# Filter loads issued as two half loads: attention and a long convolution on one core

## The chip, the cores and the metric

The kernel runs on one core of a Trainium2 chip. The core has a matrix engine (PE), a vector engine (DVE), a scalar engine (ACT), GpSimd (POOL) and a queue engine (SP) that here does nothing but issue DMAs. Sixteen DMA engines move the data; the code of the engines is fetched over them too. The metric is the time of one execution on the device in microseconds, as the median of several runs.

## The reference

Two independent parts, whose outputs stand side by side in the last dimension (2048 positions, 2 x 512 channels, bf16):

```
a = softmax((x Wq)(x Wk)^T * Dh**-0.5) (x Wv)  per head (32 heads of 16), joined, @ wo

k_shift[s] = sum_t k[s - (ks-1-t)] * shift_k[ks-1-t]      # 4 taps
kv = k_shift * v
y  = irfft(rfft(pad(kv)) * rfft(pad(ssm_k)))[:S]          # causal convolution, 2048 taps a channel
b  = q * (y + kv * ssm_D)
return concat([a, b], -1)
```

## The kernel before

**Attention.** There are 32 head pairs by query blocks of 512, each over 16 key tiles. PE computes scores into PSUM (line 910). ScalarE turns most of the score blocks into weights with the exponential (line 935, result in PT); DVE does the others with integer arithmetic (lines 1019, 1029 and 1036, result in RST). PE then multiplies the weights by the values (line 1128). This goes on for the whole span.

**Convolution.** No transform is used: the causal convolution is done by PE as products with Toeplitz blocks (`conv_lags`, line 1379). The reversed filter rows, with ssm_D added at lag zero, are stored once to a scratch tensor in HBM, `kz_scratch` (`kz_store`). A *filter load* reads them back so that partition p of a block of 64 partitions begins one element later than partition p-1, which lays out a Toeplitz block. Each of the 256 loads takes 2 x 64 = 128 rows of SEG + S//2 = 2112 elements of bf16, 4224 bytes, into one of the R_W = 9 slots of WR. Two loads make one *quad* of four channels; there are 128 quads, and four quads in a row are a burst of the convolution. For a quad PE issues 8 lags x 4 small matmuls, its first behind the landing of both loads (`h_wr[qd]`).

**The order of work.** The program is written out by a planner in Python that keeps an estimated clock for each engine. It decides at each step which of the pieces of work is issued next: scores, value products, projections, convolution lags. The instructions of an engine then run in exactly that order, and each waits on semaphores for what it needs. The DMAs of the filter are all issued by SP in order. `open_wr` puts a load on the list when the slot it writes is free (its last reader is done); `release` (line 1344) calls `feed_wr` when the planner's estimate of the load's end (`dma_t`, at WR_KB = 330 KB a microsecond) lies early enough before the time at which PE's next block of 256 instructions is to be there. The load is then tied to a place in PE's program: SP waits until PE has come there. The planner thus counts on a block of code being served behind loads that were issued before it was asked for.

**What the change touches.** `dma` (line 419) issues a transfer on an engine's queue, books it in the planner and returns the semaphore and the count to wait for; a transfer adds 16 to the semaphore. `feed_wr` makes the source pattern of a filter load (line 1336) and calls `dma` (line 1337). The semaphores `d_wr` go round by quad modulo 6. Other users of SP's queue around it are `spread_kv` (KV<-KV, a shift within SBUF in pieces of 128 bytes) and `load_v` (OUTA<-in_B_v_dram, pieces of 256 bytes).

Of the kernel before, what the change touches and what calls it, by code (L numbers as in the profile page):

```python
# [13 lines left out]
S = 2048  # L14
# [17 lines left out]
SEG = S // 2 + 64  # L32
LEFT = 16
LKR = LEFT + S
R_W = 9
# [129 lines left out]
WR_KB = 330  # L165
# [168 lines left out]
def bass_concat_heads__mha_block__ssm_conv_h3__prompt_kernel(  # L334
# [14 lines left out]
    kz_ap = nc.dram_tensor("kz_scratch", (C // 2, 2, 2 * SEG), BF16).ap()  # L349
# [7 lines left out]
    def sem(name):  # L357
        return enter(nc.semaphore(name))

    def sb(name, shape, dt=BF16):  # L360
        return enter(nc.sbuf_tensor(name, shape, dt))
# [8 lines left out]
    WR = sb("WR", [128, R_W, SEG + S // 2])  # L370
# [42 lines left out]
    act, dve, pool, sp = [Eng(sem(n), done) for n in ("s_act", "s_dve", "s_pool", "s_sp")]  # L413
    dma_t = [0.0]

    def at(*deps):
        return pe.at(deps)

    def dma(eng, dsem, outp, inp, deps=(), transpose=False, kb=512, rate=DMA_KB, late=4.2):
        h = dsem.add()  # L420
        start = max(eng.t, at(*deps))
        dma_t[0] = max(dma_t[0], start + late) + kb / rate
        if kb >= 256:
            pe.loads.append((start + 1.31, dma_t[0] - 0.85))
        done[(id(h[0]), h[1])] = dma_t[0]

        def fn(e):
            f = e.dma_start_transpose if transpose else e.dma_start
            f(outp, inp).then_inc(dsem.sem, 16)  # L429
        issue = kb / (rate if rate < DMA_KB else 155) if transpose else 0.55  # L430
        eng.op(fn, deps, inc=False, us=(issue, issue + 0.06))
        return h
# [41 lines left out]
    d_wr = [DmaSem(sem(f"d_wr{i}")) for i in range(6)]  # L474
# [5 lines left out]
    def load_x(sc, skip=0):  # L480
        t0, t1 = sc * 512 + skip, (sc + 1) * 512
        h_x[sc] = [dma(sp, d_x[sc], xT[:, :, t0:t1], x2[t0:t1, :], transpose=True, kb=t1 - t0, rate=X_KB, late=1.8)]
    h_xn = dma(sp, d_x[4], XN, x2[0:256, :].rearrange("(j p) f -> p j f", p=128), kb=256, late=1.8)
    h_wq = [dma(act, d_w[0], WQ[:, :, 0:128], wview[:, :, 0:128], kb=128, late=1.8)]
    h_wk = [dma(act, d_w[1], WK[:, :, 0:128], wview[:, :, D:D + 128], kb=128, late=1.8)]
    load_x(0, 256)
# [21 lines left out]
    src = bass.AP(tensor=k2.tensor, offset=k2[0:1, 0:1].offset, ap=[[D, S // 2], [S // 2 * D, 2], [1, D]])  # L508
# [173 lines left out]
    h_kzw = [None]  # L682
# [624 lines left out]
    h_wr, h_qn = {}, {}  # L1307
# [5 lines left out]
    def channel(qd):  # L1313
        return 256 * (qd // 64) + 128 * (qd % 2) + 8 * (qd % 64 // 4) + 4 * (qd % 4 // 2)
# [4 lines left out]
    def open_wr(k, dep, staged=False):  # L1319
        if wr_rows[0] == R_W - 2 and not staged:  # L1320
            wr_late.append((k, dep))
            return
        for n in range(wr_rows[0], min(wr_rows[0] + k, C // 2)):
            wr_todo.append((n, dep))
            if n < R_W:
                feed_wr(1)
        wr_rows[0] += k
        if staged:
            for late in wr_late:
                open_wr(*late)  # L1330

    def feed_wr(k, h=None):
        for n, dep in wr_todo[:k]:
            qd, r = n // 2, n % 2
            src = kz_ap[channel(qd) // 2 + r, 0, 0:1]
            src = bass.AP(tensor=kz_ap.tensor, offset=src.offset, ap=[[1, 64], [2 * SEG, 2], [1, SEG + S // 2]])
            h_wr[qd] = dma(sp, d_wr[qd % 6], WR[:, n % R_W, :], src, [h_kzw[0], dep, h], kb=528, rate=WR_KB, late=2.95)
            if r == 1:
                wr_next[0] = qd + 1
        del wr_todo[:k]  # L1340
# [3 lines left out]
    def release():  # L1344
        if h_out and at(h_out[0]) < pe.t - 1.0:
            load_qn(1, [h_out.pop()])
        h = (pe.sem, pe.n)
        words = BLOCK - pe.at_word % BLOCK
        ends = pe.t + words / (70.0 if busy_conv() else 33.0) + SPAN - LOADED
        while wr_todo and max(dma_t[0], max(at(h) + 0.13, sp.t) + 2.95) + 528 / WR_KB - 0.85 <= ends and pe.t >= pe.crossed + 0.6:  # L1350
            feed_wr(1, h)
# [237 lines left out]
    def tail_bank(t):  # L1589
        return 3 * ((end[0] + t) % 2) + 2  # L1590
# [14 lines left out]
    def do_piece(t, o):  # L1605
        pieces.remove((t, o))
        h = op_mm(NQB - 1, t, o, o + 1, tail_bank(t))
        if o == 3 and t < 3:
            op_out(NQB - 1, t, tail_bank(t), h)
        return h  # L1610
# [51 lines left out]
    for p in sorted(pieces):  # L1662
# [4 lines left out]
        h = do_piece(*p)  # L1667
    for i, eng in ((0, act), (1, dve)):
        sl = slice(256 * i, 256 * i + 256)
        dst, src = QT[:, 1, 0, sl], PS[:, (tail_bank(3), BGB)[i], sl]  # L1670
# [59 lines left out]
```

## Time and profile before

| | us |
|---|---|
| median of 3 runs | 719.72 (719.65 to 720.16) |
| profiled execution, own time | 722.91 |
| its span, first to last instruction | 721.1 |
| ScalarE busy | 703.4 (98%) |
| DVE busy | 691.3 (96%) |
| PE busy | 683.2 (95%) |
| mean granted clock of PE | 0.995 of full |
| median of a filter load, issue to landing | 6.2 |

All times in the views count from the first instruction of the profiled execution. "issue" as the cause of a wait means that the engine waited for nothing that the profile shows; "L1379" is line 1379 of the kernel. In the DMA views q1 is SP's queue, q0 that of GpSimd, and q8 brings PE's code in packets of 16 KB; the share is that of all 16 DMA engines in the stretch that was asked for, and can be a little over 100% because a packet counts whole in the stretch where it starts.

### The profile page before, as it was taken

Reading aid. Unit: us, or ns where it says so; the run is one execution under the profiler, and the core shown is the slowest. Engines: PE = TensorE matmul, PEld = TensorE weight load, DVE = VectorE, ACT = ScalarE, POOL = GpSimd, SP = SyncE. Lnnn points to the kernel's source line nnn. Section 1 sums busy time; section 2 is a strip of 40 time slices with the busy share of each in tenths; the row PEclk is TensorE's granted clock in tenths of the full one; section 3 lists DMA queues with packets and bytes.
Section 4 is the critical chain, followed back from the end, with each engine's and each line's share of the span. In section 5 each row is a group of like instructions: output and inputs, shape, how many; then the busy total and the mean of one; then the engine's idle time right before and its main releaser. Section 6 shows DMA issues by size and latency. Waiting matters only on the chain.

```text
span 721.1 us, 25543 instructions
## 1 busy us (share of the span) xinstructions
PE 683.2 (95%) x11264; PEld 275.0 (38%) x11264; DVE 691.3 (96%) x1313; ACT 703.4 (98%) x646; POOL 96.5 (13%) x161
## 2 busy tenths in 40 slices
PE   9999999999899999999999999999999999999988
PEld 4334334334334434434333334333333333332244
DVE  5999999999799999999999999999999999999994
ACT  7999999999799999999999999999999999999997
POOL 5200311020020201002041020100202030211001
PEclk9999999999899999999999999999999999999999
DMA  9988644778857877588987578988885874713001
GB/s 229 289 215 270 141 168 140 258 254 299 269 204 277 292 269 264 161 306 294 332 258 217 184 247 313 338 288 307 295 318 189 310 281 163 288 57 59 16 17 32
DMA packets 83045, 164.23 MB, mean 228 GB/s; under 512 B 41232, under 2 KB 47256, under 8 KB 82680
## 3 DMA queue, kind: packets, MB, share of 16 engines
q1 hardware_dynamic: 75880, 153.61, 62.4%
q0 software_dynamic: 5856, 8.66, 4.9%
q8 instruction: 90, 1.47, 0.8%
q10 hardware_dynamic: 1200, 0.33, 0.2%
q14 instruction: 19, 0.16, 0.1%
HBM read 149.17 MB, written 8.54 MB: 219 GB/s over the span
## 4 chain that ended last, share of the span: by engine, by line
ACT 49%; DVE 32%; PE 18%; issue 1%
ACT PT L935 49%; DVE RST L1019 15%; DVE RST L1036 7%; PE PS L1128 7%; PE PS L910 6%; DVE RST L1029 4%; PE PS L1379 2%; DVE YB L1395 1%; DVE DT L1220 1%; PE PS L1294 1%; DVE KV L651 1%; PE PS L583 1%; DVE VA L666 1%; DVE KTo L640 1%; DVE VS L1060 0%
## 5 line engine op out<-in xcount | busy, mean ns | idle before, releaser
L935 ACT ACTIVATE PT<-PS 128x1024 bf16<-128x1024 f32 (+1 forms) x640 | 700.5, 1266 | 8.7 <-PE PS L910 7.8
L1019 DVE TENSOR_SCALAR RST<-PS 128x512 uint16<-128x512 f32 x513 | 342.6, 679 | 4.7 <-PE PS L910 4.0
L910 PE MATMUL PS<-QT,KTo 32*128 32x512 bf16 (+2 forms) x2248 | 257.6, 365 | 30.6 <-ACT PT L935 8.4
L1128 PE MATMUL PS<-PT,VA 128*32 128x512 bf16 (+2 forms) x1696 | 279.9, 367 | 0.3 <-issue 0.2
L1128 PE MATMUL PS<-RST,VS 128*32 128x512 bf16 (+1 forms) x1656 | 242.2, 370 | 0.3
L1036 DVE TENSOR_SCALAR RST<-RST 128x2048 uint16<-128x2048 uint16 x257 | 173.9, 681 | 0.6
L910 PEld LDWEIGHTS PS<-QT,KTo 32*128 32x128 bf16 x2248 | 67.9, 91 | 215.8 <-ACT PT L935 131.9
L1128 PE MATMUL PS<-RST,VA 128*32 128x512 bf16 (+1 forms) x552 | 123.7, 372 | 0.9 <-DVE DT L1220 0.7
L429 POOL DMA_DIRECT2D QT<-QS x120 | 65.6, 555 | 432.5 <-DVE QS L631 390.5
L1029 DVE TENSOR_SCALAR RST<-RST 128x1024 uint16<-128x1024 uint16 x257 | 101.6, 415 | 0.6
L1128 PEld LDWEIGHTS PS<-PT,VA 128*32 128x32 bf16 x1696 | 68.9, 94 | 79.4 <-issue 57.1
L1379 PE MATMUL PS<-WR,KV 128*28 128x128 bf16 (+7 forms) x4096 | 99.1, 221 | 0.0
L1379 PEld LDWEIGHTS PS<-WR,KV 128*30 128x30 bf16 (+7 forms) x4096 | 77.4, 101 | 27.9 <-issue 7.4
L1128 PEld LDWEIGHTS PS<-RST,VS 128*32 128x32 bf16 x1656 | 59.1, 95 | 53.6 <-issue 31.3
L1584 PE MATMUL PS<-IDN,ZW 128*32 128x256 bf16 (+3 forms) x150 | 37.9, 301 | 0.2
L1128 PEld LDWEIGHTS PS<-RST,VA 128*32 128x32 bf16 x552 | 30.8, 95 | 14.2 <-issue 7.2
L1220 DVE STREAM_TRANSPOSE DT<-PS 128x512 f32<-128x512 f32 x31 | 22.0, 709 | 3.8 <-PE PS L1128 3.5
L1395 DVE CAST YB<-PS 128x512 bf16<-128x512 f32 x32 | 21.8, 680 | 1.4 <-PE PS L1379 0.8
L429 POOL DMA_DIRECT2D out_dram<-OUTA x15 | 11.4, 759 | 62.5 <-DVE OUTA L1302 62.5
L1294 PE MATMUL PS<-WKV,OTN 128*128 128x512 bf16 (+1 forms) x68 | 18.9, 371 | 0.3 <-DVE OTN L1269 0.3
L615 PE MATMUL PS<-WKV,xT 128*128 128x128 bf16 x256 | 18.6, 220 | 0.5 <-DVE KTo L640 0.4
L592 PE MATMUL PS<-xT,WKV 128*128 128x512 bf16 (+1 forms) x64 | 16.7, 376 | 0.4
(72 smaller groups left out, 252.1 us busy)
## 6 DMA issues: line engine op xcount, KB each, us to landing
WR<-kz_scratch SPq DMA_DIRECT2D x256, 528.0 KB, 6.2
kz_scratch<-WR SPq DMA_DIRECT2D x4, 544.0 KB, 4.7
kt_scratch<-in_B_k_dram SPq DMA_DIRECT2D x1, 2048.0 KB
QN<-in_B_q_dram POOLq DMA_DIRECT2D x4, 512.0 KB, 7.0
out_dram<-QN POOLq DMA_DIRECT2D x4, 512.0 KB, 6.9
QT<-QS POOLq DMA_DIRECT2D x120, 16.0 KB, 3.4
out_dram<-OUTA POOLq DMA_DIRECT2D x15, 128.0 KB, 2.2
QN<-in_B_ssm_k_dram SPq DMA_DIRECT2D x1, 1024.0 KB, 8.2
```

Source lines behind the costliest of these rows:

```text
L429: f(outp, inp).then_inc(dsem.sem, 16)
L910: ins = e.matmul(PS[:, bank, i * w:i * w + w], lhsT=KTo[32 * s:32 * s + 32, OF[n_] % 2, kt * 128:(kt + 1) * 128], rhs=QT[32 * s:32 * s + 3 ...
L935: h_exp[T] = act.op(lambda e: e.activation(PT[:, p0:p0 + n, :].rearrange("p b f -> p (b f)"), PS[:, banks[0]:banks[0] + n, :].rearrange("p ...
L1019: st["h"].append(urgent(lambda e: e.tensor_scalar(lin[:, 0, half, :].bitcast(U16), PS[:, bank, :], FIX_ADD, FIX_HI, ALU.add, ALU.min), [h, ...
L1029: st["s"][0] = dve.op(lambda e: e.tensor_scalar(both(lin, 1, 2).bitcast(U16), both(lin, 0, 1).bitcast(U16), SHIFTS[0], None, ALU.add), [st ...
L1036: st["s"][1] = dve.op(lambda e: e.tensor_scalar(both(dst, 0, 2).bitcast(U16), both(lin, 0, 2).bitcast(U16), SHIFTS[1], None, ALU.add), [st ...
L1128: ins = e.matmul(dst, lhsT=w, rhs=rhs, start=first, stop=last, tile_position=(0, 32 * s))
L1220: h_t = urgent(lambda e: e.transpose(out=dt, in_=PS[:, PVB, :]), [h, h_mul.get(n - 1)], slack=S_T, us=(0.63, 0.751))
L1294: ins = e.matmul(PS[:, b, c0:c1], lhsT=OTN[:, PAIRS.index((o, qb)), t * 128:(t + 1) * 128], rhs=WO[:, o, c0:c1], start=(o == 0), stop=(o = ...
L1379: ins = e.matmul(dst, lhsT=KV[:, channel(qd) // 4, 2 * n:2 * NB, g], rhs=WR[:, (2 * qd + g // 2) % (R_W), w0:w0 + 128], start=(n == 0), st ...
L1395: bank_free[BGB] = h_ybw[0] = urgent(lambda e: e.tensor_copy(YB[:, qd % 8 // 4, :], src), [h, h_yb[0]], slack=S_C, us=V512)
L1584: pe.op(lambda e, s=s, dst=dst, rhs=rhs, rows=rows, first=first: e.matmul(dst, lhsT=ZW[:, 0:rows], rhs=rhs, start=first, stop=first, tile_ ...
```

## The change

`dma` takes lists of outputs and inputs and issues one transfer for each pair, each with its own 16 on the same semaphore; the count that is returned is that of the last. `feed_wr` gives it two halves of the columns, w = 1056 elements (2112 bytes) each. The planner books one load of 528 KB as before, so all compute engines get the same instructions in the same order, and the waits have other counts only.

```diff
     def dma(eng, dsem, outp, inp, deps=(), transpose=False, kb=512, rate=DMA_KB, late=4.2):
-        h = dsem.add()
+        parts = list(zip(outp, inp)) if isinstance(outp, list) else [(outp, inp)]
+        for _ in parts:
+            h = dsem.add()
...
-            f(outp, inp).then_inc(dsem.sem, 16)
+            for o, i in parts:
+                f(o, i).then_inc(dsem.sem, 16)
...
             src = kz_ap[channel(qd) // 2 + r, 0, 0:1]
-            src = bass.AP(tensor=kz_ap.tensor, offset=src.offset, ap=[[1, 64], [2 * SEG, 2], [1, SEG + S // 2]])
-            h_wr[qd] = dma(sp, d_wr[qd % 6], WR[:, n % R_W, :], src, [h_kzw[0], dep, h], kb=528, rate=WR_KB, late=2.95)
+            w = (SEG + S // 2) // 2
+            src = [bass.AP(tensor=kz_ap.tensor, offset=src.offset + w * i, ap=[[1, 64], [2 * SEG, 2], [1, w]]) for i in range(2)]
+            h_wr[qd] = dma(sp, d_wr[qd % 6], [WR[:, n % R_W, w * i:w * i + w] for i in range(2)], src, [h_kzw[0], dep, h], kb=528, rate=WR_KB, late=2.95)
```

## The prediction

> **What bounds the kernel now.** I read the page first (busy shares, DMA queues and issues), then the waits of all engines and of the SP queue, then the DMA traffic of single stretches, then the timeline at the places where those pointed.
>
> The page:
> ```profile
> span 721.1 us, 25543 instructions
> ...
> PE 683.2 (95%) x11264; PEld 275.0 (38%) x11264; DVE 691.3 (96%) x1313; ACT 703.4 (98%) x646; POOL 96.5 (13%) x161
> ...
> q1 hardware_dynamic: 75880, 153.61, 62.4%
> ...
> WR<-kz_scratch SPq DMA_DIRECT2D x256, 528.0 KB, 6.2
> ```
> The waits (who waited for whom: us in total, times, longest), of the engines and then of the SP queue:
> ```profile
> PEld PS L910 <- ACT PT L935: 131.9, 324, 0.9
> ...
> PEld PS L1379 <- issue: 7.4, 30, 0.4
> ...
> PE PS L910 <- issue: 2.3, 2, 1.8
> ```
> ```profile
> SPq L429 <- PE PS L910: 368.0, 118, 19.5
> ```
>
> ScalarE is busy for 703.4 of 721.1 us, and DVE and PE have little more room: a microsecond in which PE stands still is a microsecond lost, apart from PE's lead. That lead is the wait of PE's weight load for ScalarE, 131.9 us in 324 waits, 0.41 us each. No row of the waits names the landing of a filter load: the convolution (line 1379) waits for nothing but issue, 0.4 us at most. The loads are thus hidden now. But they are 256 x 528 KB, nearly all of the SP queue's traffic, and the question is how much cover they have.
>
> **The price of a half load.** What follows are the DMA traffic of five stretches (queue: packets, MB, share of 16 engines), and the issues of the fourth and the fifth.
>
> 46 to 50 us, the writing of kz_scratch in pieces of 2176 bytes:
> ```profile
> q1 hardware_dynamic: 774, 1.58, 103.7%
> ```
> 62 to 68 us, filter loads alone:
> ```profile
> q1 hardware_dynamic: 582, 2.19, 90.8%
> ```
> 188 to 190.4 us, pieces of 256 bytes:
> ```profile
> q1 hardware_dynamic: 1985, 0.49, 91.4%
> ```
> 410 to 545 us:
> ```profile
> q1 hardware_dynamic: 10294, 38.62, 80.2%
> ...
> q8 instruction: 18, 0.29, 0.8%
> ...
> WR<-kz_scratch SPq DMA_DIRECT2D x70, 528.0 KB, 6.4
> ```
> ```profile
> L429 SPq DMA_DIRECT2D WR<-kz_scratch x70: 512/556/1121, 412.3 to 535.0; - x70
> ```
> 474 to 486 us:
> ```profile
> q1 hardware_dynamic: 1136, 4.26, 94.5%
> ```
> ```profile
> 474.17 11.52 SPq L429 DMA_DIRECT2D WR<-kz_scratch  x7
> ```
>
> A filter load is 128 rows of 2112 bf16, 4224 bytes each, and moves 0.541 MB. Unhurried (62 to 68) a MB takes 0.908 x 6 / 2.19 = 2.49 us of the 16 engines, so a load 1.345 us; in the crowded stretch 0.802 x 135 / 38.62 = 2.80 us, so 1.52. After the change the rows are 2112 bytes. The nearest row is the kz_scratch write, 2176 bytes a piece: 1.037 x 4 / 1.58 = 2.63 us a MB, so 1.42 a load, 0.075 above 1.345. The 256-byte row agrees: 0.914 x 2.4 / 0.49 = 4.48 us a MB is 2.0 more than 2.49 for some 3700 more pieces, 0.54 ns a piece spread over 16 engines; 128 more pieces a load make 0.07. Bounds: from below, 2.63 beside the crowded 2.80 a MB would be a gain of 0.09 us a load; from above, each load could pay the difference of 1.52 and 1.345 once more, 0.17. I take 0.075 because the piece is nearly the same size as in the row, though that one writes HBM. Over 256 loads it is 19 us of DMA time beside the compute engines.
>
> The Trainium skill (DMA: Bandwidth & Descriptors, "Why small descriptors are slow (HBM only)") puts a fixed cost of about 3 cycles on each packet beside one cycle per 32 bytes. By it the halves would be 138 cycles for 135, 2%, an estimate of 0.03 us a load, and all three terms below would shrink to about four tenths; the rows give 5.5%, and I keep them.
>
> **The change part by part.** Removed is nothing; all compute instructions and their waits stay in their order. Added are 256 issues on SP and a second count of 16 on the semaphore, which the convolution waits for; the last half to land now decides.
>
> SP: an issue takes 0.51 to 0.61 us (median 556 ns), so 256 more make 143 us, and SP waits 368 us for PE at line 910 alone. In the densest row 7 loads took 11.52 us; 14 halves of 0.61 are 8.5, so SP keeps up. What is behind in its queue comes later only in a burst: n loads keep SP 0.6 n us longer. That is hidden where the DMA engines are still behind (1.42 us a load, SP 1.2); a lone load's second half starts 0.6 us later, and its two halves of 0.7 us land about when the whole one does. If that cover is gone, 0.6 us a load comes on top. POOL's and ScalarE's queues are not touched, but their transfers share the engines, with q0 below 2% in the crowded stretch.
>
> Crowding: from 410 to 545 a load is asked for each 135 / 70 = 1.93 us and q1 fills 80.2%; plus 70 x 0.075 = 5.3 us it fills 84%, and from 474 to 486 it goes from 94.5 to 94.5 + 7 x 0.075 / 12 = 99%. With 6.4 us from issue to landing, 3.3 loads are under way at a time, so a landing comes about 0.25 us later, and more in bursts.
>
> First term, the one place where PE visibly waits for code. The timeline:
> ```profile
> 174.97 3.97 SPq L429 DMA_DIRECT2D WR<-kz_scratch  x5
> 181.78 0.62 SPq L429 DMA_DIRECT2D KV<-KV  x1
> ...
> 189.00 0.60 PE L910 MATMUL PS<-QT,KTo 32*128 32x512 bf16 x1 [1.78 <-issue]
> ```
> ScalarE's waits from 186 to 196 us:
> ```profile
> ACT PT L935 <- PE PS L910: 3.6, 4, 1.9
> ```
> The DMA traffic from 182 to 186.6 us, and from 186.6 to 187.6:
> ```profile
> q1 hardware_dynamic: 2020, 1.45, 97.3%
> ```
> ```profile
> q8 instruction: 1, 0.02, 5.5%
> ```
> And the stretch after it (busy times of the engines, granted clock, DMA share, GB/s):
> ```profile
> 189.00:195.50 6.50, 6.50 (x74) 2.48 (x75) 3.11 (x7) 4.16 (x4) 0.00 (x0) 0.50 0.79 234
> ```
>
> PE stands 1.78 us with no semaphore behind it. From 182 to 186.6 the q1 row shows 97.3% and no q8 packet; the one 16 KB packet of instructions comes between 186.6 and 187.6. So a block of PE's code is served behind the loads and copies already queued. Afterwards the granted clock is 0.50 for 6.5 us, and ScalarE loses 3.6 us in four waits (186 to 196 us). With five loads ahead the block comes 5 x 0.075 = 0.4 us later, nothing covers that: **+0.4** (0.15 to 0.9).
>
> Second term, the tightest convolutions. The first row is SP's burst around them (328 to 348 us); the next two rows are the load issued at 335.9 with its neighbour, then the one at 344.6, then the convolutions that need them (two loads a quad, counted in order: quads 59 and 61):
>
> ```profile
> 328.82 16.26 SPq L429 DMA_DIRECT2D WR<-kz_scratch  x11
> ```
> ```profile
> L429 SPq DMA_DIRECT2D WR<-kz_scratch x2: 606/606/606, 335.3 to 335.9; - x2
> ...
> DMA to landing us min/median/max: 7.5/8.7/9.9
> ```
> ```profile
> L429 SPq DMA_DIRECT2D WR<-kz_scratch x1: 512/512/512, 344.6 to 344.6; - x1
> ...
> DMA to landing us min/median/max: 8.3/8.3/8.3
> ```
> ```profile
> 346.54 0.25 PE L1379 MATMUL PS<-WR,KV 128*32 128x128 bf16 x4
> ...
> 353.33 0.73 PE L1379 MATMUL PS<-WR,KV 128*32 128x128 bf16 x40
> ```
>
> 335.9 + 9.9 = 345.8, used at 346.54: 0.7 us to spare. 344.6 + 8.3 = 352.9, used within the run from 353.33 to 354.06: 0.4 to 1.2. About seven loads since 328.8 pay 0.5 us, and a burst of four keeps SP 2.4 us longer, of which the queue hides all or most. So each place loses between nothing and 1.5 us, less PE's lead of 0.4; a stall in the first also gives the second time. I take **+0.6** together (0 to 2.5).
>
> Third term, the other code blocks. 18 blocks to 70 loads make 66 beside 256 loads, each about 0.25 us later. Only two waits for issue before line 910's matmuls sum to 2.3, so nearly all blocks arrive in time now; the page does not show by how much. If none had spare time: 66 x 0.25 = 16.5, half of it within PE's lead, 8; if all had, nothing. With one in ten on the edge 1.65, half hidden: **+0.8**.
>
> Sum: 0.4 + 0.6 + 0.8 = 1.8 us. The profiled execution took 722.91 us (1.8 beyond its span, 3.2 above the median); it would take 724.7. On the median of 719.72 this gives 721.5.
>
> **The rivals.** *No measurable change*: the loads have spare time at the second and third places, and only the first term remains: 720.1. For it: no wait for a landing in the whole profile; against it: 0.7 us at quad 59 and 94.5% at 474. The Trainium skill (Runtime: NRT & Kernel Launch, "Instruction fetch mechanics") calls the fetch of the next 16 KB block mostly hidden; by that this rival would win, but the 1.78 us disagree.
>
> *Faster*: the halves hold SP back, so less is queued ahead of a code block. Place: the stall at 189. SP's burst of five loads would end at 174.97 + 10 x 0.61 = 181.1, with a code block that holds SP about 182, and KV<-KV and the two loads behind it (OUTA) move back; if PE's block is asked for before them, the stall and its slow clock go, 3.6 us: 716.1. It decides from the point where KV<-KV is issued after the request. Against it: the five loads themselves are still ahead, and the q1 row is full before 181.78 matters. The Trainium skill (DMA: Bandwidth & Descriptors, "Queues, rings and completion order") lets an engine turn between queues after each packet; then a code block would hardly wait for loads. No q8 packet before 186.6 under 97.3% of q1 speaks for a wait.
>
> *Much slower*: the half costs 0.17 or more. Then 474 to 486 asks for 94.5 + 9.9 = 104%, the DMA engines bound such stretches, and each 12 us lose 0.5 or more; over the 135 us from 410 and the crowded part before, some 200 us, 8 us: 728.
>
> **How the numbers follow.** Within 0.2% is 718.28 to 721.16, about what a measurement of this kernel can tell from no change. Chances: slower by waits as summed 0.40, centre 721.5, own range 720.7 to 724; no measurable change 0.33; much slower 0.14; faster 0.13. A tenth or so of the first ends below 721.16, and as much of the second above, which cancel. So slower 0.54, same 0.33, faster 0.13. The range, 718.8 to 728, leaves out most of the faster case and half of the much slower one, 0.2 together.
>
> **What would show it.** q1's share from 410 to 545 near 84% shows the price; the median from issue to landing of the second halves shows the queue; the wait before 189 us longer than 1.78 shows the first term, a wait of line 1379 or 910 for issue near 346 us the second, more waits for issue above 0.5 us the third. The prediction is wrong if halves are no dearer than whole rows, if the stall near 189 is gone, or if SP's spacing, not the engines, sets the landings.

## The result and the profile after

| | before | after |
|---|---|---|
| median of 20 runs, us | 719.67 (718.33 to 723.69) | 721.70 (719.93 to 723.92) |
| ratio of the two, with 95% interval | | 1.0029 (1.0018 to 1.0040) |
| profiled execution, own time, us | 722.91 | 720.96 |
| its span, us | 721.1 | 719.2 |

The changed kernel is slower by 0.29%, 2 us. The profiled execution of it is nevertheless the shorter of the two. That is no contradiction: the 20 executions of each kernel lie 4 to 5.4 us apart, and the profile of before happened to hold a long stall near 189 us. Medians and intervals say what the change costs; a single profile only says where time can be lost.

The page of the changed kernel:
```profile
span 719.2 us, 25799 instructions
...
PE 681.6 (95%) x11264; PEld 274.9 (38%) x11264; DVE 691.1 (96%) x1313; ACT 703.2 (98%) x646; POOL 96.3 (13%) x161
...
q1 hardware_dynamic: 112744, 153.62, 65.8%
...
WR<-kz_scratch SPq DMA_DIRECT2D x512, 264.0 KB, 4.7
```
Its waits (us in total, times, longest), of the engines and then of the SP queue:
```profile
PEld PS L913 <- ACT PT L938: 133.0, 327, 0.9
...
PEld PS L1383 <- issue: 6.7, 28, 0.4
...
PE PS L913 <- issue: 1.3, 3, 0.6
...
PEld PS L1383 <- DMA WR<-kz_scratch: 0.3, 1, 0.3
```
```profile
SPq L432 <- PE PS L913: 207.9, 99, 17.4
```
The lines of the kernel have moved by three or four (429 is now 432, 910 is 913, 935 is 938, 1379 is 1383). ScalarE is still the busiest. One row names the landing of a filter load, 0.3 us for a weight load of the convolution, where none did before. SP now waits 207.9 us for PE at line 913, where it was 368.0: the second issues have eaten 160 us of its idle time.

The DMA traffic from 410 to 545 us (queue: packets, MB, share of 16 engines), and SP's issues in it:
```profile
q1 hardware_dynamic: 20202, 37.92, 82.3%
...
WR<-kz_scratch SPq DMA_DIRECT2D x140, 264.0 KB, 4.8
```
```profile
L432 SPq DMA_DIRECT2D WR<-kz_scratch x140: 512/606/1722, 409.8 to 544.6; - x140
```
The engines' time for a load can be read from this: 0.823 x 135 / 37.92 = 2.93 us a MB, where it was 2.80; times 0.541 MB that is 0.07 us more a load. Over the whole span 65.8% of 719.2 is 473.2 us and 62.4% of 721.1 was 450.0: 23 us over 256 loads, 0.09 each. An issue on SP takes 606 ns in the median, and up to 1722.

**The place near 189 us.** SP's queue from 172 to 195 us (start, length, tile, count), then PE's row after the gap, and the stretch from 189 (busy times of the engines, granted clock, DMA share, GB/s):
```profile
171.42 11.75 SPq L432 DMA_DIRECT2D WR<-kz_scratch  x14
183.21 0.62 SPq L432 DMA_DIRECT2D KV<-KV  x1
183.88 5.52 SPq L432 DMA_DIRECT2D OUTA<-in_B_v_dram  x2
```
```profile
188.81 0.38 PE L913 MATMUL PS<-QT,KTo 32*128 32x512 bf16 x1 [0.61 <-issue]
```
```profile
189.00:195.50 6.50, 6.34 (x100) 2.71 (x100) 5.70 (x12) 6.27 (x5) 0.00 (x0) 1.00 0.87 242
```
PE waits 0.61 us where it waited 1.78, and the clock stays at 1.00 where it fell to 0.50.

**The place of the second term.** The one wait for a landing is at quad 59, which the prediction had named. The load's last half, and the convolution's first weight loads:
```profile
L432 SPq DMA_DIRECT2D WR<-kz_scratch x1: 606/606/606, 336.2 to 336.2; - x1
...
DMA to landing us min/median/max: 7.4/7.4/7.4
```
```profile
343.71 0.47 PEld L1383 LDWEIGHTS PS<-WR,KV 128*32 128x32 bf16 x32 [0.32 <-DMA WR<-kz_scratch]
```
The half lands at 343.67 us and is used at 343.71: the 0.7 us to spare are gone. PE loses little by it. From its last scores to the convolution it is 0.42 us (343.29 to 343.71), where it was 0.32 before (346.22 to 346.54).

**A new place.** PE's row near 460 us, and the DMA traffic from 454 to 457.6 and from 457.6 to 458.7 us:
```profile
459.91 0.40 PE L1131 MATMUL PS<-PT,VA 128*32 128x512 bf16 x3 [0.86 <-DVE RST L1022]
```
```profile
q1 hardware_dynamic: 644, 1.21, 92.6%
```
```profile
q1 hardware_dynamic: 194, 0.36, 100.6%
q8 instruction: 1, 0.02, 5.7%
```
The row puts the 0.86 us down to DVE. But until 457.6 us no packet of q8 comes, under 92.6% of q1, and then one comes: PE again stood for a block of its code that was served behind filter loads. In the profile before, PE runs through this place.

### The profile page after: what moved, and what is told of

It reads as the page before. It is cut to its first block, busy times and chain, and to the rows that moved or that the text cites. A ratio compares the mean times of both kernels' runs of the same rounds, so it can differ in the third digit from the quotient of the medians.

```text
span 719.2 us, 25799 instructions
## 1 busy us (share of the span) xinstructions
PE 681.6 (95%) x11264; PEld 274.9 (38%) x11264; DVE 691.1 (96%) x1313; ACT 703.2 (98%) x646; POOL 96.3 (13%) x161
## 3 DMA queue, kind: packets, MB, share of 16 engines
q1 hardware_dynamic: 112744, 153.62, 65.8%
## 4 chain that ended last, share of the span: by engine, by line
ACT 51%; DVE 32%; PE 16%; issue 1%
ACT PT L938 51%; DVE RST L1022 15%; DVE RST L1039 7%; PE PS L1131 6%; PE PS L913 5%; DVE RST L1032 4%; PE PS L1383 1%; DVE YB L1399 1%; DVE DT L1223 1%; PE PS L586 1%; PE PS L1297 1%; DVE KV L654 1%; DVE VA L669 1%; DVE VS L1063 1%; PE PS L726 1%
## 5 line engine op out<-in xcount | busy, mean ns | idle before, releaser
L1383 PEld LDWEIGHTS PS<-WR,KV 128*28 128x28 bf16 (+7 forms) x4096 | 77.0, 101 | 27.5 <-issue 6.7
```

What stands on the lines that cost most here:

```text
L1383: ins = e.matmul(dst, lhsT=KV[:, channel(qd) // 4, 2 * n:2 * NB, g], rhs=WR[:, (2 * qd + g // 2) % (R_W), w0:w0 + 128], start=(n == 0), st ...
```

## The experiments

Three theories stood against each other. The *engines*: the smaller pieces, or the greater number of DMAs, cost DMA time. The *issues*: SP needs a second issue of 0.6 us for each load, so the end of a burst moves towards the moment at which PE asks for a block of its code. *One place*: the stall near 189 us decides alone. A "request" below is taken to be the moment when PE enters a new block of its program, found by counting its instructions in order.

### The change once more

> The changed kernel once more, for a second profile. Theory A (the pieces: 2112-byte rows cost the DMA engines some 0.08 to 0.09 us more a load, so landings and code blocks come later): about 721.7 us, SP's queue at 65 to 66% of the DMA engines' span, and waits of PE for issue that fall at other code blocks than in the first profile. Theory B (the issues: SP spaces the halves, and the second half decides the landing): the same time. Theory C (one place, the stall near 189 us, decides): the time of the profiled execution goes with whether PE stands there.

The file is the changed kernel itself. Median 722.58 us (721.0 to 725.74, 12 runs) beside 719.83 for before (29 runs), ratio 1.0044 (1.0025 to 1.0063). The slowdown is there again. Its profiled execution lost time elsewhere. PE's row near 578 us:
```profile
577.78 0.39 PE L913 MATMUL PS<-QT,KTo 32*128 32x512 bf16 x3 [0.90 <-ACT PT L938]
```
PE stood 0.90 us there and hardly at 189. Which places stall differs from execution to execution. Not all of it is due to filter loads: at the same instruction of PE this execution is 2.2 us behind the last section's already at 30 us, and the first filter load is issued after 55.

### Two issues with whole rows

```diff
-            w = (SEG + S // 2) // 2
-            src = [... offset=src.offset + w * i, ap=[[1, 64], [2 * SEG, 2], [1, w]]) for i in range(2)]
+            src = [... offset=src.offset + 2 * SEG * i, ap=[[1, 64], [1, SEG + S // 2]]) for i in range(2)]
-            h_wr[qd] = dma(sp, ..., [WR[:, n % R_W, w * i:w * i + w] for i in range(2)], src, ...)
+            h_wr[qd] = dma(sp, ..., [WR[i:128:2, n % R_W, :] for i in range(2)], src, ...)
```

> Each load as two issues, one of the even and one of the odd partitions, with whole rows of 4224 bytes: 256 more issues, no more row pieces. Theory A: SP's queue stays at 62.4 to 63% and the time within 0.2% of 719.7. Theory B: slower by 1.5 to 2.5 us, as the halves.

722.28 us (719.83 to 723.88), ratio 1.0028 (1.0011 to 1.0044): as slow as the halves, although no piece is smaller than before. The page's row of SP's queue:
```profile
q1 hardware_dynamic: 79976, 153.62, 65.2%
```
65.2% of the span of 718.4 is 468.4 us, 18.4 above the 450.0 of before, 0.07 a load. The 5% more packets are 16 of 4 bytes for each second DMA, 9 ns each in the mean, 0.01 us a load. The rest is that a row's packet takes 196 ns here in the mean, where it took 188 before. Why is not shown; each DMA of this kernel writes every second partition, and no run separates that. Smaller pieces are not needed for the slowdown.

### Two issues, rows in two pieces, without the unused columns

The source and the destination of `rows`, with each row cut into two pieces of 1024 columns, and the 64 columns that the products do not read (1024 to 1087) left out.

```diff
+            src = [... offset=src.offset + 2 * SEG * i, ap=[[1, 64], [SEG, 2], [1, S // 2]]) for i in range(2)]
```

> As the last, two issues by even and odd partitions, but each row in two pieces of 2048 bytes (64 columns that no convolution reads, 1024 to 1087, are left out, 3% of the bytes). Theory A: SP's queue at about 64.5% (65.8% less 3% of the bytes, plus the fixed part), slower than before by 0.5 to 2 us. Theory B: the same as whole rows in two issues.

721.55 us (718.51 to 725.23), ratio 1.0013 (0.9995 to 1.0032): between the two, and not to be told from either. Its row shows the most engine time of the kernels with two issues:
```profile
q1 hardware_dynamic: 112744, 149.43, 67.5%
```
67.5% of 719.5 is 485.7 us, 35.7 above before, and yet it isn't slower than the halves with their 23. That speaks against the engines' time as the cause, but not sharply.

### A second issue that moves 32 bytes

```diff
+            d_tny.add()
+            sp.op(lambda e, n=n: e.dma_start(TNY[:, n:n + 1], q2[0:16, n:n + 1], ...).then_inc(d_tny.sem, 16), [], inc=False, us=(0.0, 0.0))
```

> The kernel before, and behind each filter load a second issue on SP that moves 16 elements of 2 bytes to a tile nobody reads: SP's extra work without the bytes. Theory A (what counts is the DMA engines' time): SP's queue stays near 62.4%, the time within 0.2% of 719.8 us. Theory B (what counts is that SP gives out one load in 1.2 us, not in 0.6): slower by 1.5 to 2.5 us.

721.45 us (719.76 to 725.27), ratio 1.0030 (1.0015 to 1.0046): the whole slowdown, with the loads left as they were. The page's row of the queue, the row of the added issues (ns, least, median and most), and PE's row near 578 us:
```profile
q1 hardware_dynamic: 84072, 153.63, 63.1%
```
```profile
L1341 SPq DMA_DIRECT2D TNY<-in_B_q_dram x256: 311/592/2074, 55.7 to 630.6; - x128
```
```profile
578.91 0.39 PE L912 MATMUL PS<-QT,KTo 32*128 32x512 bf16 x3 [1.28 <-ACT PT L937]
```
63.1% of 722.0 is 455.6 us: 0.02 us of engine time a load, a quarter of the halves' price. What the two kernels share is the issue of about 0.6 us on SP between one load and the next. The stall at 578 us is a new one: in the profile before, PE passes there without a gap. Near 189 PE stands 1.51 us in this execution.

### Half the bytes, in one issue and in two

From the tenth load on only the left half of the columns is loaded, so part of the convolution works on old columns; the work of all compute engines is the same.

```diff
+            w = SEG + S // 2 if n < R_W else (SEG + S // 2) // 2          # narrow1, one issue
+            w = (SEG + S // 2) // (2 if n < R_W else 4)                   # narrow2, two issues of w columns
```

> The kernel before, but from the tenth load on only the left half of the columns is loaded, in one issue: half the bytes, the same issues. The right half of each slot keeps old data, so the convolution of part of the channels is left wrong. Theory A: crowding is gone, SP's queue at 36 to 38%, no block of code waits behind loads any more: faster than before by 1 to 4 us. Theory B: within 0.2% of before.

> As the last, with the same half of the columns, in two issues of 528 columns: twice the issues, half the bytes (part of the convolution left wrong in the same way). Theory A: like the last within 0.2%, since the DMA engines have room for both. Theory B: slower than the last by 1.5 to 2.5 us.

One issue: 718.01 us (717.27 to 719.18), ratio 0.9975 (0.9964 to 0.9986). Two: 718.46 (717.54 to 719.25), ratio 0.9980 (0.9964 to 0.9995). The rows of SP's queue, of the first kernel and of the second, and ScalarE's waits in the second:
```profile
q1 hardware_dynamic: 75880, 86.83, 40.5%
```
```profile
q1 hardware_dynamic: 112744, 86.85, 44.7%
```
```profile
ACT PT L938 <- PE PS L913: 3.8, 12, 0.6
```
With the engines half empty the second issue costs 0.45 us, not to be told from nothing by the spread of the runs, where it cost 2. PE waits for issue nowhere longer than 0.4 us. The engine time that the split adds is not smaller here: 0.447 x 716.4 - 0.405 x 716.5 = 30 us over 247 loads, 0.12 each. So neither the issues nor their engine time costs much by itself; they cost in a crowded queue. The pair also shows what half the bytes gain: about 1.7 us.

### Three and four issues a load

```diff
-            w = (SEG + S // 2) // 2
+            w = (SEG + S // 2) // 3        # thirds; // 4 in quarters, with range(3) and range(4)
```

> Three issues a load, of 704 columns each. SP needs 3 x 0.6 = 1.8 us a load where 1.93 us are there on average from 410 to 545 us, and two loads in a burst come closer than that. If SP's spacing costs: much more than twice the cost of the halves, 725 to 745 (ratio 1.008 to 1.035), below the quarters' 883, since SP can still just keep up. If the engines' time for pieces or the number of DMAs costs: twice the halves' 2 us, 723.5 to 724.5 (ratio 1.005 to 1.007).

> Each load in four issues of 528 columns (1056 bytes a row). Theory A: three times the added pieces, so 0.27 us more a load, 69 us in all, SP's queue at 72%, crowded stretches near 95%: slower by 5 to 12 us. Theory B: SP needs 4 x 0.6 = 2.4 us a load where 1.93 us are there from 410 to 545 us, so SP bounds such stretches: slower by 25 us or more, with SP's issues back to back.

Thirds: 756.18 us (753.29 to 760.15), ratio 1.0502 (1.0466 to 1.0539). Quarters: 883.39 (881.48 to 888.04), ratio 1.2274 (1.2239 to 1.2309). PE's wait for landings in the thirds, then in the quarters, and the quarters' SP queue from 400 to 460 us:
```profile
PE PS L1383 <- DMA WR<-kz_scratch: 25.4, 20, 3.4
```
```profile
PE PS L1383 <- DMA WR<-kz_scratch: 105.4, 46, 6.4
```
```profile
400.01 60.01 SPq L432 DMA_DIRECT2D WR<-kz_scratch  x82
```
82 issues stand back to back in 60 us: 0.73 us each, 2.9 us for a load of four, where one is asked for each 1.93 us. Here SP is the bound and the convolution waits for landings, where with one or two issues a single wait of 0.3 us is all. The expectation for four (25 us or more) held; that for three was too low even by the SP theory (745 at most). 3 x 0.606 is still 1.82 us, but some issues are held, and SP needs 136.6 us for the 183 issues from 409.6 us on, 2.24 us a load. The engines are not full in either: q1 fills 78.0% from 410 to 545 us with three issues, 59.2% from 400 to 460 with four. Over one issue a load, two cost 2 us, three 36 and four 164.

### Loads tied to an earlier place

```diff
+            if h is not None:
+                first = max(at(h) - 0.6, pe.crossed + 0.6)
+                early = max([v for v in range(max(n0, pe.n - 200, 1), h[1]) if at((pe.sem, v)) <= first], default=h[1])
+                ...      # SP waits for `early` instead of h
```

> The halves, with the place in PE's program to which a load is tied moved forward by about 0.6 us, the time of the second issue, wherever the slot is already free and the place stays 0.6 us behind the request of a code block (about half of the 247 loads that are tied to a place). Number of DMAs, their pieces and the order on all compute engines are those of the changed kernel. If the spacing of SP's issues is what costs (the last half of a burst comes 0.6 us or more later ahead of a code block): 719.4 to 720.6, ratio 0.9995 to 1.0012, and the block near 571 us begins as early as in the kernel before. If the pieces or the number of DMAs cost by themselves: 721.5, ratio 1.0025 or more, as the changed kernel. If the queue alone sets when a load ends, an earlier issue changes nothing either: 721.5.

> The kernel before (one issue a load) with the same loads tied to the same earlier places. If the last issues ahead of a code block decide whether PE stalls: faster than before, 718.4 to 719.3, ratio 0.998 to 0.9994, bounded below by 718.0, the time with half the bytes. If the queue alone sets it, or the stalls come from elsewhere: 719.7, ratio 1.000 within 0.1%.

The halves, tied earlier: 722.25 us (718.21 to 726.29), ratio 1.0027 (1.0008 to 1.0046). The kernel before, tied earlier: 721.83 (720.08 to 725.02), ratio 1.0021 (1.0002 to 1.0040). I had expected that earlier loads would cure the one and speed up the other. Neither happened; the kernel before became slower (the interval only just leaves out no change), with no DMA added and no piece changed. 164 of its 256 loads are issued more than 0.3 us earlier on PE's clock. The place near 577 us shows how that can cost. First the kernel before: SP's load in question, the packet of PE's code (DMA traffic from 575.44 to 575.50 us), and PE's rows:
```profile
L429 SPq DMA_DIRECT2D WR<-kz_scratch x1: 513/513/513, 574.4 to 574.4; - x1
...
DMA to landing us min/median/max: 5.5/5.5/5.5
```
```profile
q8 instruction: 1, 0.02, 102.0%
```
```profile
577.54 0.38 PE L1128 MATMUL PS<-RST,VS 128*32 128x512 bf16 x1
577.86 0.39 PE L910 MATMUL PS<-QT,KTo 32*128 32x512 bf16 x3
```
Then the same with loads tied earlier (the traffic from 575.7 to 575.8 us):
```profile
L429 SPq DMA_DIRECT2D WR<-kz_scratch x1: 514/514/514, 571.9 to 571.9; - x1
...
DMA to landing us min/median/max: 4.8/4.8/4.8
```
```profile
q8 instruction: 1, 0.02, 60.0%
```
```profile
576.26 0.38 PE L1128 MATMUL PS<-RST,VS 128*32 128x512 bf16 x1
577.90 0.40 PE L910 MATMUL PS<-QT,KTo 32*128 32x512 bf16 x3 [1.27 <-ACT PT L935]
```
The same row of PE stands at 577.54 and at 576.26, so the second execution is ahead by 1.28 us. Put on the first one's clock, its load is issued at 573.2 instead of 574.4, and the block of code comes at about 577.0 instead of 575.4. The load landed 3.4 us behind the end of the block's packet before (579.9 and 576.4), and lands with it now (576.7 both): it went ahead of the block. The matmul that follows, due at 576.58, starts at 577.90. It is put down to ScalarE, but ScalarE itself was waiting for PE then (its waits from 574 to 579 us):
```profile
ACT PT L935 <- PE PS L910: 1.0, 1, 1.0
```
What came last was the block. One load more ahead of it goes with 1.3 us of PE standing still. The five loads before it also came 0.2 to 0.8 us earlier, so the price of this one alone is not isolated. In the halves with the same move PE stood longer at this place than in any other profile:
```profile
578.64 0.61 PE L913 MATMUL PS<-QT,KTo 32*128 32x512 bf16 x3 [2.64 <-issue]
```

So my reading of *issues* as "later is worse" fell: earlier can be worse too. What counted here is whether a load is served ahead of the block. It is tempting to say that the request draws the line, but it doesn't here: it is at 571.69 us before and at 570.41 with earlier ties, and in both the load is issued after it, by 2.7 and by 1.5 us. At which moment a load can no longer get ahead of the block is not shown. That moving issues in time is enough to change the time, without more of them, is what these runs show; that the second issue does its harm in the same way is likely, but argued from single places.

### Transfers put behind the block near 182 us

```diff
-        h_kvc[c] = dma(sp, d_kvc[c], dst, src, [hh, h_kv0, h_kvc[c - 1] if c else None], kb=256, rate=KV_KB)
+        h_kvc[c] = dma(sp, d_kvc[c], dst, src, [hh, h_kv0, h_kvc[c - 1] if c else None, (pe.sem, pe.n + 11) if c == 2 else None], kb=256, rate=KV_KB)
```

> The kernel before (one issue a load); only the shift KV<-KV of the third channel group, and with it the two OUTA loads and everything behind them on SP, waits in addition for a place in PE's program 11 counted instructions later, some 4 us, so that PE asks for its block of code near 182 us before these transfers are issued. If transfers issued ahead of the block's request are what PE waits for at 187 to 189 us: that stall and its slow clock are absent, the block starts about 1.5 us or less after the crossing instead of 3.0 to 4.5, and the median falls by what the stall costs in the average execution, 0.3 to 1.5 us: 718.2 to 719.4 (ratio 0.998 to 0.9996). If the five filter loads ahead are enough for the wait: the block starts as late as before and the time stays at 719.7. If the loads behind on SP have no spare time: a new wait of the convolution for a landing near 195 to 205 us and 720.5 or more.

718.97 us (717.40 to 721.04, 12 runs) beside 719.57, ratio 0.9993 (0.9979 to 1.0007): in the direction of a gain, not to be told from none. SP's queue from 172 to 195 us, the DMA traffic from 185 to 186.2, and ScalarE's waits from 184 to 196:
```profile
175.13 3.94 SPq L429 DMA_DIRECT2D WR<-kz_scratch  x5
185.27 0.62 SPq L429 DMA_DIRECT2D KV<-KV  x1
185.93 1.75 SPq L429 DMA_DIRECT2D OUTA<-in_B_v_dram  x2
```
```profile
q1 hardware_dynamic: 28, 0.09, 18.3%
q8 instruction: 1, 0.02, 4.8%
```
```profile
ACT PT L935 <- PE PS L910: 0.3, 1, 0.3
```
The packet of code comes between 185 and 186.2 us, where the profile before had it between 186.6 and 187.6, and ScalarE loses 0.3 us there instead of 3.6. But it still comes 2.9 us after the request (4.5 before), with only the five loads ahead of it, not 1.5 as I had expected. And a second profile of the unchanged kernel, 719.83 us, shows hardly a stall there either:

> The kernel before once more, for a second profile. If the stall near 189 us belongs to the program, PE stands there again for 1.5 to 2 us with the clock at half behind it; if it comes and goes, the profiled execution is 2 to 4 us shorter.

In that execution PE stood 0.97 us at 385 us instead. SP's row of the KV shift, ScalarE's waits from 184 to 196 us, and PE's row at 385:
```profile
181.38 0.62 SPq L429 DMA_DIRECT2D KV<-KV  x1
```
```profile
ACT PT L935 <- PE PS L910: 0.4, 1, 0.4
```
```profile
385.45 0.39 PE L910 MATMUL PS<-QT,KTo 32*128 32x512 bf16 x2 [0.97 <-issue]
```
Between the two profiles of one program the stalls moved by 200 us of the span; so the 3.6 us that the first profile shows at 189 are not what the average execution pays there. The two also answer the question of this section in part. In both, KV<-KV is issued 0.37 us ahead of the request, with the same five loads before it; yet the packet comes 4.5 us after the request in the one and 3.0 in the other. The order of issue alone does not decide whether the block is late.

## Why the prediction was right, and where it was not

The time was forecast as 721.5 us and is 721.7; slower was the likeliest sign. By its own steps:

- **The price of a half load, 0.075 us of engine time.** This held, with its reason: 0.07 from 410 to 545 us (q1 at 82.3% with 0.7 MB less moved, where 84% was forecast), 0.09 over the span. In the trace a row's packet takes 188 ns in the mean before, and a half row's 99 after: 10 ns more a row, 0.08 us a load over 16 engines. The estimate of 0.03 that I worked out from the Trainium skill (DMA: Bandwidth & Descriptors, "Why small descriptors are slow (HBM only)") is below that. But this time is not what made the kernel slower.
- **"SP keeps up", and its longer bursts are hidden.** This step failed. SP does keep up with two issues (207.9 us of waits for PE are left), but what it does meanwhile is not hidden: a second issue with 0.02 us of engine time costs the whole 0.3%. The prediction had named SP's spacing as what would make it wrong, and for the cause it did.
- **First term, the stall at 189 us, +0.4.** Not borne out. PE waited 0.61 us there in the profile after instead of 1.78. Across the kernels that place stalls in some executions and not in others, the unchanged kernel included, so what it costs on average stays open.
- **Second term, the tight convolutions, +0.6.** Right in kind, far too large. At quad 59 the spare 0.7 us went and the convolution waited for the landing, in the one profile of the halves and not in the other; PE lost 0.1 us by it. At quad 61 no wait shows.
- **Third term, the other code blocks, +0.8.** With so little in the other two this one is left to carry the 2 us, and it was too small. New waits for a block of code appear in the halves at 460 us (0.86) and at 577 (0.90), and with the tiny issue at 577 (1.28). But the profiles do not add up to 2 us. Between 100 and 700 us, compared at the same instructions of PE, the two profiles of before lose 5.1 and 2.5 us against the kernel with half the bytes in one issue, and the two of the halves 2.4 and 2.3. That all 2 us are of this kind is the likeliest reading, not a measurement.
- **The clock** had no term of its own. It isn't the main part: among executions with a mean granted clock of 1.000, the 63 of before have a mean of 719.5 us and the 14 of the halves one of 721.3. But a clock of 0.998 or less shows in 14 of all 32 executions of the halves, and in 17 of the 98 of before that ran beside the experiments.
- **The sum** came out right by luck: of the 1.0 us in the first two terms the runs show about 0.1, and the third term, if it carries the rest, was too small by about as much.
- **The rivals.** *No measurable change* (720.1, ratio 1.0005) is excluded by the interval (1.0018 at the least). Its premise, that there is spare time at the other places, fails at quad 59, at 460 and at 577 us. *Faster*: its mechanism did occur. KV<-KV is issued at 183.21 us, just behind PE's request at 183.19, where before it was 0.37 us ahead, and the stall is short; but the unchanged kernel shows a short one too with KV<-KV 0.37 us ahead, so this is not shown to be why. *Much slower* by full engines did not come; the cliff is on SP's side, and begins at three issues.
- On the turn between queues, the Trainium skill (DMA: Bandwidth & Descriptors, "Queues, rings and completion order") says that an engine goes round the queues that have work, packet by packet. A block that was asked for at 452.9 us and comes only after 457.6, under 92.6% of q1, does not fit a short turn; the measurement decides here.

What stays open: whether the tiny issue costs by SP's time alone or also by its own packets in the queue, why a block is late in one execution and not in the next under the same issues, and how the 2 us are spread over the places. Issuing the second halves from another engine's queue was not tried.

## What to carry to other kernels

Where an engine fetches its code over the same DMA engines as the data, count DMA issues as a resource of their own: with a queue near 80% full in its crowded part a second issue of 0.6 us per load cost 0.3% while moving only 32 bytes, and loads in three issues cost 5%, in four 23%. Ask of every transfer near a code block whether it is served ahead of it; at one place a load that got ahead went with a stall of 1.3 us. And when single executions differ by more than the effect, let medians of many runs say how much, and profiles only where.

## What the hardware showed that I had not expected

- After the packet of its code landed, PE resumed only 1.2 to 1.6 us later: in the run with loads tied earlier the packet ends at 576.71 and the matmul starts at 577.90; in the profile before 187.57 and 189.00, with the tiny issue 187.82 and 189.43 (ends of single q8 packets in the trace).
- What a stall costs depends on the clock behind it. PE stood 1.51 us near 189 in the halves with earlier ties and with the tiny issue. In the 6.5 us after it the granted clock was 1.00 in the one and 0.74 in the other, and from 150 to 200 us they lost 1.6 and 2.8 us against the kernel with half the bytes in one issue. The 1.78 us of before, with 0.50 behind them, came to 4.4.
- An issue on SP that takes 0.5 to 0.6 us is held now and then: up to 1.7 us with the halves and 2.07 in the run with tiny issues. The held ones mostly stand beside a packet of PE's code: in the profile after, 39 of the 43 issues of filter loads over 0.9 us overlap a q8 packet, of the other 469 only 51.
- Two DMAs of whole rows, each to every second partition, took 0.07 us more of the engines' time than one with the same rows, of which the second DMA's own packets are 0.01.
- Halving the bytes of nearly all loads, in a kernel where no engine ever waits for one, gained 1.7 us. The blocks of code came earlier there: 1.0 us after the request in the mean of 78 blocks, where it is 2.2 in both profiles of before, 2.4 and 2.5 with the halves and 2.5 with the tiny issue (from the starts of the q8 packets and PE's instructions counted in order). With one issue tied earlier it is 2.0, though that kernel was slower: the mean does not decide.
